# The small tail of an expert computed in front of its last full group of tokens

## The chip, the core and the metric

The kernel runs on one core of a Trainium2 chip. Its time is the device time of one execution in microseconds (us), the median of several runs. A core has five engines, each with its own queue of instructions that it works through in order: PE (matrix products; its weight loads are listed apart as PEld), DVE (vector operations), ACT (activation functions and copies), POOL (here nearly all indirect DMAs) and SP (here only DMAs). They wait for each other by semaphores, which a program sets from the data that instructions read and write.

## The reference

An attention with a local window and block summaries makes `x`, 3072 tokens of 512 numbers. Then a mixture of eight experts follows, of which each token uses two:

```python
logits = x @ w_gate
noisy_logits = logits + np.log1p(np.exp(x @ w_noise)) * noise
top2 = np.argpartition(-noisy_logits, 2, axis=1)[:, :2]
...
for e in range(E):
    for k in range(2):
        mask = top2[:, k] == e
        h = np.maximum(x[mask] @ w1[e], 0.0)
        out[mask] += top2_w[mask, k, None] * (h @ w2[e])
```

`w1[e]` is 512 x 1024 and `w2[e]` 1024 x 512. Only the experts matter here.

## The kernel before

The first 200 us or so compute the attention and the gate, which sorts the tokens of each expert into a list. After that the experts follow one another, in the order of how many tokens they have. Their numbers of places are fixed by `CAPS = (800, 832, 808, 800, 784, 776, 768, 768)`. All numbers are split in two float16 parts, high and low, so that a product of two matrices takes three passes: high by high, low by high, high by low.

From expert 2 on, an expert `e` goes through two stages:

- **First product** (`h = relu(x w1)`), `seven`: the expert's tokens are cut in two halves of `h = CAPS[e] // 2` columns, and `w1` in blocks, so that seven block products in place of eight make the result. One call `seven(e, i, u)` makes product `u` for block `i` with six matmuls (L1359), about 1 us. DVE and ACT add the products up (L1380 to L1387) and write `h` into the buffers `hth` and `htl` (high and low part, L1391 and L1394).
- **Second product** (`h w2`), `mm2_part`: for each group `c` of 128 tokens, 24 matmuls of 128 x 512 (L1431), about 5.2 us, into a PSUM buffer `pt` of which there are two. What lies beyond six groups of 128 is the **tail**, `c = LAST = 6`. Experts 3, 4 and 5 have tails of 32, 16 and 8 tokens (`four(e, c)` is true for them): 24 matmuls with 32 columns each, four side by side in the array (L1425), about 1.5 us for all, whose four partial sums then lie in four strips of 32 partitions. Experts 1 and 2 have larger tails (64 and 40 tokens), 6 and 7 have none.

`mm2_out` ends a group: one DVE instruction (L931) multiplies by the gate's weight and adds the tokens' old output rows, which `prev_gather` has fetched into one of three buffers `prev`; then POOL scatters the result to `out` (L90). For a tail of at most 32 tokens it is four DVE instructions, one for each strip, each adding to the one before (L920).

To have PE busy between two experts, `seven_head(n)` makes products 1 and 5 of the next expert `n = e + 1` ahead of the last turn of expert `e`. These twelve matmuls are called **the head** here. Product 1 writes the tile that PE rows call `o`, product 5 one called `h`.

The order of everything else is written out by hand: between PE's pieces of work the program calls `hook(t)`, and `on(t, f, ...)` puts a call at number `t`. In the second product the numbers are `32 + 3 * c` and `33 + 3 * c`, behind the first and the second pass of group `c`, and `34 + 3 * c`, behind its `mm2_out`. So a call's number fixes its place on its engine, and every engine keeps to that order. What the change touches:

- `plan_x(n, 3, 32, (44, 44, 44), (45, 45), (46, 46, 46, 46))` prepares the next expert's own tail for the first product: at most 16 rows of `x` are gathered, DVE makes three sums (L1292 to L1296, number 44), ACT the high parts (L1312, number 45), DVE the low parts (L1322, number 46, that is behind group 4), and for each part SP issues a DMA transpose (L1328) that puts it into the columns which the head reads too. The low parts of expert 4 lie in the tile `xl`, those of expert 5 in `xte`. Experts 6 and 7 have no tail, so nothing of this is done for them.
- `plan_w1(n, 3, 38, 47, 47, 48, 48, 49)` prepares the last quarter of the next expert's `w1`: four sums on DVE (L1339, number 47), the high parts on ACT (L1348, 47 and 48), the low parts on DVE (L1352, 48 and 49). They read staging buffers `stg`, four of them, which the next loads of weights reuse: the last two quarters of `w2` of expert `n` (L735 on SP, called early in the next expert), which ACT and DVE then split (L740, L758).
- `on(43, xs_gather, n + 1, 0)` and `on(47, xs_gather, n + 1, 1)` fetch token rows for the expert after next, by POOL.

The second product's loop before: groups 0 to 5 in order, then the tail, and the head ahead of whatever comes last.

Of the kernel before, what the change touches and what calls it, by code (L numbers as in the profile page):

```python
# [25 lines left out]
E, F = 8, 1024  # L26
# [37 lines left out]
def attn_moe(ctx, tc, qt, kt, vt, wgn, noise, w1, w2, out):  # L64
# [23 lines left out]
    def indirect(**kw):  # L88
        nc.gpsimd.memset(spacer, 0.0)
        return nc.gpsimd.indirect_dma_start(**kw)  # L90


    LAST = NCH - 1
# [74 lines left out]
    for i in range(3):  # L168
        m = const.tile([P, W], BF, name=f"mask{i}")
# [128 lines left out]
    def bank():  # L298
        return banks[0].tile([P, 1, 512], F32, name="h")
# [480 lines left out]
    def four(e, c):  # L780
        return c == LAST and CAPS[e] - LAST * P <= 32

    def tb_of(e, c):
        return TB0[:, c] if e == 0 and c < 3 else TB[:, e, c]
# [3 lines left out]
    def chunks(e):  # L788
        return -(-CAPS[e] // P)
# [83 lines left out]
    def prev_gather(e, c):  # L873
        n = min(P, CAPS[e] - c * P)
        pv = PREV[pi_[0] % len(PREV)]
        pi_[0] += 1
        if c == LAST and not four(e, c):
            g = indirect(
                out=pv[:, :HD], out_offset=None, in_=out2,
                in_offset=bass.IndirectOffsetOnAxis(ap=IL[:, e:e + 1], axis=0),  # L880
                bounds_check=2 * N - 1, oob_is_err=False)
        else:
            g = indirect(
                out=pv[:n], out_offset=None, in_=out,
                in_offset=bass.IndirectOffsetOnAxis(ap=tb_of(e, c)[:n, 0:1], axis=0),
                bounds_check=N - 1, oob_is_err=False)
        for o in ow.get(e, []):
            tc.declare_no_dep(g.ins, o.ins, reason="an expert's slots hold different tokens")
        ow.setdefault(e, []).append(g)
        return pv  # L890
# [20 lines left out]
    def mm2_out(e, c, py, pv):  # L911
        last = c == LAST
        if four(e, c):
            n = CAPS[e] - LAST * P
            y = late[0].tile([P, DM], F32, name="y", bufs=4)[:n]
            gw = tb_of(e, c).bitcast(F32)[:n, 1:2]
            for g in range(4):
                x = py[32 * g:32 * g + n]
                if g or pv is not None:
                    nc.vector.scalar_tensor_tensor(y, x, gw, y if g else pv[:n], op0=OP.mult, op1=OP.add)  # L920
                else:
                    nc.vector.tensor_scalar(y, x, gw, None, op0=OP.mult)
            y_scatter(e, c, y)
            return
        d = HD if last else DM
        y = late[0].tile([P, DM], F32, name="y", bufs=4)[:, :d]
        gw = (TL[:, e] if last else tb_of(e, c)).bitcast(F32)[:, 1:2]
        if pv is None:
            nc.vector.tensor_scalar(y, py[:, :d], gw, None, op0=OP.mult)
        else:  # L930
            nc.vector.scalar_tensor_tensor(y, py[:, :d], gw, pv[:, :d], op0=OP.mult, op1=OP.add)  # L931
        y_scatter(e, c, y)
# [287 lines left out]
    py = [bank()[:, 0] for c in range(3)]  # L1220
# [242 lines left out]
    def on(t, f, *a):  # L1463
        plan.setdefault(t, []).append((f, a))

    def hook(t):
        for f, a in plan.pop(t, []):
            f(*a)

    def plan_w1(n, p, t, *u):  # L1470
        on(t, w_load, n, p)
        on(u[0], w1_sums, n, p)
        for i in range(2):
            on(u[1 + i], w1_hi, n, p, i)
        for i in range(2):
            on(u[3 + i], w1_lo, n, p, i)
# [10 lines left out]

    for e in range(1, E):
        pv = []

        def prev():
            if len(pv) < chunks(e):
                pv.append(prev_gather(e, len(pv)))

        n = e + 1
        if e == 1:
            on(0, tail_ids)
            plan_x(n, 0, 0, (3, 3, 3), (4, 4), (5, 5, 5, 5))
            plan_x(n, 1, 1, (6, 6, 6), (7, 7), (8, 8, 8, 8))
            plan_w1(n, 0, 1, 9, 9, 10, 10, 10)  # L1500
            plan_w1(n, 1, 2, 11, 11, 12, 12, 12)
            plan_x(n, 2, 7, (13, 13, 13), (14, 14), (15, 15, 15, 15))
            plan_w1(n, 2, 11, 33, 33, 34, 34, 34)
            plan_x(n, 3, 12, (35, 35, 35), (36, 36), (37, 37, 37, 37))
            plan_w1(n, 3, 13, 38, 38, 39, 39, 39)
        else:
            for i, (a, b) in enumerate(((3, 4), (4, 7), (8, 14), (15, 21))):
                on(a, w_hi, e, 4 + i)
                on(b, w_lo, e, 4 + i)
            on(36, tail_next, e)  # L1510
            if n < E:
                plan_x(n, 0, None, (9, 11, 12), (10, 13), (15, 16, 18, 19))
                plan_x(n, 1, None, (22, 23, 25), (24, 27), (28, 29, 29, 31))
                plan_w1(n, 0, 8, 32, 32, 33, 33, 34)
                plan_w1(n, 1, 15, 35, 35, 36, 36, 37)
                plan_x(n, 2, 20, (38, 38, 38), (39, 39), (40, 40, 40, 40))
                plan_w1(n, 2, 35, 41, 41, 42, 42, 43)
                plan_x(n, 3, 32, (44, 44, 44), (45, 45), (46, 46, 46, 46))
                plan_w1(n, 3, 38, 47, 47, 48, 48, 49)
            if e > 2:  # L1520
                on(4, w_load, e, 6)
                on(4, w_load, e, 7)
        if n + 1 < E:
            on(40 if e == 1 else 43, xs_gather, n + 1, 0)
            on(42 if e == 1 else 47, xs_gather, n + 1, 1)
        if n < E:
            on(44, w_load, n, 4)
            on(44, w_load, n, 5)
        if e == 1:
            on(48, w_load, n, 6)  # L1530
            on(48, w_load, n, 7)
        for t in (17, 20, 23):
            on(t, prev)
        if e == 1:
            for half in range(2):
                for f in range(FC):
                    mm1(e, half, f)
                    hook(8 * half + f)
            for t in range(16, 32):
                hook(t)  # L1540
        else:
            hi, lo = seven(e, 0, 2)
            hi()
            lo()
            hook(3)
            seven(e, 0, 6)
            for t in range(4, 7):
                hook(t)
            for i in range(1, 5):
                if i < 4:  # L1550
                    seven(e, i, 1)
                    hook(7 * i)
                    seven(e, i, 5)
                    hook(7 * i + 1)
                h7 = seven(e, i - 1, 7)
                h7[0]()
                hook(7 * i + 2 if i < 4 else 28)
                if i < 4:
                    h2 = seven(e, i, 2)
                    h2[0]()  # L1560
                    h7[1]()
                    hook(7 * i + 3)
                    seven(e, i, 6)
                    h2[1]()
                    hook(7 * i + 4)
                else:
                    py = psum.tile([P, 512], F32, name="pt", bufs=2)
                    mm2_part(e, 0, py, 0, range(7), True, False)
                    h7[1]()
                    hook(29)  # L1570
                h3 = seven(e, i - 1, 3)
                h3[0]()
                hook(7 * i + 5 if i < 4 else 30)
                h4 = seven(e, i - 1, 4)
                h4[0]()
                h3[1]()
                h4[1]()
                hook(7 * i + 6 if i < 4 else 31)
        for c in range(chunks(e)):
            if c == chunks(e) - 1 and n < E:  # L1580
                seven_head(n)
            if c or e == 1:
                py = psum.tile([P, 512], F32, name="pt", bufs=2)
                for i, k in enumerate((0, 2, 1)):
                    if e == 1:
                        mm2_pass(e, c, py, k, 1)
                    else:
                        mm2_part(e, c, py, k, range(FC), i == 0, i == 2)
                    if i < 2:
                        hook(32 + 3 * c + i)  # L1590
            else:
                for k in (2, 1):
                    mm2_part(e, 0, py, k, range(7), False, False)
                    hook(33 - k // 2)
                for k in (0, 2, 1):
                    mm2_part(e, 0, py, k, (7,), False, k == 1)
            mm2_out(e, c, py, pv[c])
            prev()
            hook(34 + 3 * c)
        for t in range(60):  # L1600
            hook(t)
# [104 lines left out]
```

## Time and profile before

| | |
|---|---|
| median of 3 runs | 644.59 us (644.32 to 644.63) |
| the profiled execution | 642.6 us, of which the span of instructions is 640.8 |
| granted PE clock, mean | 0.997 |
| 24 matmuls of a group, L1431 | 5.2 us |
| 24 matmuls of a tail of at most 32 tokens, L1425 | 1.4 us |
| four instructions L920 on DVE | 3.1 us |
| one L931 on DVE | 0.75 us |
| the five passages from an expert to the next, 2 to 3 up to 6 to 7 | near 332, 394, 455, 516 and 572 us of the span |

The profile is of one execution. A timeline's row gives the start of a group of like instructions, its length, and what they were; in square brackets stands how long the engine sat idle ahead of it, and what ended that. Matmuls are pipelined: one of 128 x 512 is listed with 0.38 us, while the next starts 0.22 after it. So the distance of starts says how PE moves, and the length of a row ends a little after the next has begun.

### The profile page before, as it was taken

How to read it: one execution, taken by the hardware profiler on the slowest of the kernel's cores; microseconds unless marked ns; L12 is line 12 of the kernel's file. 1: busy time of each engine (PE TensorE's matmuls, PEld its weight loads, DVE VectorE, ACT ScalarE, POOL GpSimd, SP SyncE). 2: the span in 40 equal slices, each digit the busy share in tenths (PEclk: the TensorE clock that was granted, in tenths of full speed). 3: DMA queues.
4: the chain of work that ended last, by engine and by line, in shares of the span. 5: the costliest groups of instructions: out<-in, count | busy, mean ns of one | idle time of the engine just before them, and what ended most of it. 6: DMA issues, size and time to landing. Idle time of an engine off the chain costs nothing.

```text
span 640.8 us, 14153 instructions
## 1 busy us (share of the span) xinstructions
PE 622.5 (97%) x5295; PEld 358.8 (56%) x5295; DVE 481.3 (75%) x1039; ACT 315.9 (49%) x692; POOL 249.0 (39%) x432
## 2 busy tenths in 40 slices
PE   8999999999999999999999999999999999999995
PEld 7778777765654544555455544554554455445542
DVE  5768999889796797188868887987898679757410
ACT  4868988941253553075437534654464255425200
POOL 4442224203254324532573266336523532333041
PEclk9999999999999999999999999999999999999998
DMA  9999986788379976547886597759677767763021
GB/s 308 333 292 351 292 266 201 222 318 250 118 217 171 253 186 170 211 122 140 209 265 152 131 228 245 181 133 250 201 189 156 218 205 166 182 198 105 3 96 51
DMA packets 123708, 127.93 MB, mean 200 GB/s; under 512 B 83242, under 2 KB 86674, under 8 KB 123630
## 3 DMA queue, kind: packets, MB, share of 16 engines
q1 hardware_dynamic: 111838, 90.66, 53.3%
q0 software_dynamic: 11792, 36.27, 18.0%
q8 instruction: 44, 0.72, 0.5%
q14 instruction: 34, 0.28, 0.1%
HBM read 81.85 MB, written 25.61 MB: 168 GB/s over the span
## 4 chain that ended last, share of the span: by engine, by line
PE 82%; DVE 6%; issue 3%; DMA 3%; ACT 2%; POOL 1%; SPq 1%; POOLq 0%; DVEq 0%; ACTq 0%
PE pt L1431 29%; PE h L1359 16%; PE h L854 8%; PE pt L909 5%; PE pt L341 3%; PE pt L1359 3%; PE o L1359 3%; PE s L318 3%; PE o L354 3%; PE h L909 2%; DMA xte<-x 2%; PE pt L378 1%; PE o L246 1%; DVE y L920 1%; DVE htl L1394 1%
## 5 line engine op out<-in xcount | busy, mean ns | idle before, releaser
L90 POOL DMA_INDIRECT out_dram<-y,tb x52 | 69.3, 1333 | 169.4 <-DVE y L931 131.6
L90 POOL DMA_INDIRECT xg<-xd,tb x54 | 60.1, 1112 | 118.1 <-DVE dsc L653 32.3
L1431 PEld LDWEIGHTS <-hth 128*128 128x128 f16 x576 | 56.4, 98 | 66.7
L931 DVE SCALAR_TENSOR_TENSOR y<-pt,tb,prev 128x512 f32<-128x512 f32 x42 | 31.5, 750 | 67.4 <-PE pt L1431 49.8
L1359 PEld LDWEIGHTS <-w1h 128*128 128x128 f16 x504 | 48.9, 98 | 38.0 <-issue 4.1
L1431 PE MATMUL pt<-w2h,hth 128*128 128x512 f16 x288 | 69.0, 379 | 0.0
L1431 PE MATMUL pt<-w2h,htl 128*128 128x512 f16 x288 | 69.0, 379 | 0.0
L1431 PE MATMUL pt<-w2l,hth 128*128 128x512 f16 x288 | 69.0, 379 | 0.0
L1359 PEld LDWEIGHTS <-w1l 128*128 128x128 f16 x504 | 49.3, 98 | 34.9
L90 POOL DMA_INDIRECT prev<-out_dram,tb x45 | 52.4, 1165 | 23.7 <-issue 12.8
L333 ACT ACTIVATE p<-s,nm 128x120 f32<-128x120 f32 x192 | 51.0, 376 | 0.8
L854 PE MATMUL h<-xte,w1h 128*128 128x384 f16 (+2 forms) x248 | 48.9, 336 | 1.1 <-DMA xte<-x 1.1
L1431 PEld LDWEIGHTS <-htl 128*128 128x128 f16 x288 | 28.2, 98 | 34.0
L1348 ACT ACTIVATE w1h<-stg 128x768 f16<-128x768 f32 (+1 forms) x24 | 22.7, 944 | 37.9 <-DVE stg L1339 37.9
L1391 ACT ACTIVATE hth<-h 128x384 f16<-128x384 f32 (+4 forms) x48 | 23.8, 496 | 35.6 <-PE h L1359 35.6
L1348 ACT ACTIVATE w1l<-stg 128x768 f16<-128x768 f32 (+1 forms) x24 | 22.5, 942 | 37.2 <-DVE stg L1339 37.2
L1359 PE MATMUL h<-xte,w1h 128*128 128x384 f16 (+4 forms) x180 | 39.7, 329 | 0.7 <-DVE h L1385 0.4
L1359 PE MATMUL h<-xte,w1l 128*128 128x384 f16 (+4 forms) x180 | 39.7, 329 | 0.0
L1339 DVE TENSOR_TENSOR stg<-stg 128x256 f32<-128x256 f32 x96 | 36.2, 419 | 0.8
L854 PEld LDWEIGHTS <-w1h 128*128 128x128 f16 x256 | 24.7, 98 | 20.5 <-issue 2.2
L1312 ACT ACTIVATE x<-xt 128x512 f16<-128x512 f32 (+2 forms) x44 | 26.3, 625 | 19.6 <-issue 17.3
L1394 DVE SCALAR_TENSOR_TENSOR htl<-h,hth 128x384 f16<-128x384 f32 (+4 forms) x48 | 26.3, 562 | 11.8 <-ACT hth L1391 11.5
(301 smaller groups left out, 1292.0 us busy)
## 6 DMA issues: line engine op xcount, KB each, us to landing
stg<-in_w_dram SPq DMA_DIRECT2D x64, 512.0 KB
q<-in_qt_dram SPq DMA_DIRECT2D x24, 256.0 KB
xd<-x SPq DMA_DIRECT2D x24, 256.0 KB
out_dram<-xg SPq DMA_DIRECT2D x8, 768.0 KB
kb<-in_kt_dram SPq DMA_DIRECT2D x6, 768.0 KB
hth<-in_vt_dram SPq DMA_DIRECT2D x12, 260.0 KB
htl<-in_vt_dram SPq DMA_DIRECT2D x16, 195.0 KB
ve<-in_vt_dram SPq DMA_DIRECT2D x12, 260.0 KB
```

Source lines behind the costliest of these rows:

```text
L90: return nc.gpsimd.indirect_dma_start(**kw)
L333: nc.scalar.activation(PE_[t][:, a, hp, :], SC[t][:, a, hp, :], AF.Exp, bias=NM[t][:, 1, a, hp:hp + 1], scale=0.125)
L854: nc.tensor.matmul(ph[:, :n], w1_of(w, wn, c, f), x[:, xo + c, c0:c1], start=(k == 0), stop=(k == 11))
L909: nc.tensor.matmul(py, hx[:, f, c * P:c * P + P], wv[:, f, :], start=st, stop=sp)
L931: nc.vector.scalar_tensor_tensor(y, py[:, :d], gw, pv[:, :d], op0=OP.mult, op1=OP.add)
L1312: nc.scalar.activation(t[:r, c:c + k], src, AF.Copy)
L1339: nc.vector.tensor_tensor(o, x, y, op=op)
L1348: nc.scalar.activation(hi, x, AF.Copy, scale=W1S)
L1359: nc.tensor.matmul(ph[:, :h], w[:, la, a, P * j:P * j + P], x[:, j, :h], start=start and k == 0, stop=k == 5, skip_group_check=True)
L1391: nc.scalar.activation(hh[:, f, t], src, AF.Relu)
L1394: nc.vector.scalar_tensor_tensor(hl[:, f, t], src, 0.0, hh[:, f, t], op0=OP.max, op1=OP.subtract)
L1431: nc.tensor.matmul(py, x, wv[:, f, :], start=st, stop=sp, skip_group_check=True)
```

## The change

For experts whose tail has at most 32 tokens (3, 4 and 5), the last two turns of the second product change places: groups 0, 1, 2, 3, 4, then the tail, then group 5. The head of the next expert stays ahead of the last turn, which is now group 5. The fetches of old output rows follow the new order. And for these three experts the numbers of the last quarter of `w1` are written anew, since the tail's numbers (50, 51) now come ahead of those of group 5 (47, 48): its sums and high parts sit in the tail's turn, its low parts in that of group 5.

```diff
     for e in range(1, E):
         pv = []
+        turns = list(range(chunks(e)))
+        if chunks(e) > LAST and four(e, LAST):
+            turns[-2:] = turns[:-3:-1]
 
         def prev():
             if len(pv) < chunks(e):
-                pv.append(prev_gather(e, len(pv)))
+                pv.append(prev_gather(e, turns[len(pv)]))
...
-                plan_w1(n, 3, 38, 47, 47, 48, 48, 49)
+                plan_w1(n, 3, 38, *((50, 50, 51, 47, 48) if LAST in turns[:-1] else (47, 47, 48, 48, 49)))
...
-        for c in range(chunks(e)):
-            if c == chunks(e) - 1 and n < E:
+        for m, c in enumerate(turns):
+            if c == turns[-1] and n < E:
                 seven_head(n)
...
-            mm2_out(e, c, py, pv[c])
+            mm2_out(e, c, py, pv[m])
```

The order on PE where it passes from expert 3 to expert 4, before: the end of group 5 (L1431), the first and the last of the head's matmuls (L1359), the start of the tail (L1425).

```order
L1431 LDWEIGHTS htl
L1431 MATMUL pt<-w2h_321,htl 128x512
L1359 LDWEIGHTS w1h_319
L1359 MATMUL o<-xte,w1h_319 128x392
...
L1359 MATMUL h<-xl,w1h_319 128x392
L1425 LDWEIGHTS hth
L1425 MATMUL pt<-w2h_321,hth 32x512
```

And the same place after the change:

```order
L1425 LDWEIGHTS htl
L1425 MATMUL pt<-w2h_321,htl 32x512
L1359 LDWEIGHTS w1h_319
L1359 MATMUL o<-xte,w1h_319 128x392
...
L1359 MATMUL h<-xl,w1h_319 128x392
L1431 LDWEIGHTS hth
L1431 MATMUL pt<-w2h_321,hth 128x512
```

The head now stands between the tail and group 5, where it stood between group 5 and the tail.

The order on DVE at the same place, as a difference (`-` before, `+` after), from the low parts of expert 4's tail (L1322) and the sums of its `w1` (L1339) to the first results of expert 4:

```order
 L1322 TENSOR_TENSOR x<-xt,x 16x512 x2
 L1339 TENSOR_TENSOR stg<-stg 128x256 x4
+L920 SCALAR_TENSOR_TENSOR y<-pt,tb,prev_2965 32x512
+L920 SCALAR_TENSOR_TENSOR y<-pt,tb,y 32x512 x3
 L1352 SCALAR_TENSOR_TENSOR w1l_2957<-stg,w1l_2957 128x768
-L931 SCALAR_TENSOR_TENSOR y<-pt,tb,prev_2965 128x512
 L1352 SCALAR_TENSOR_TENSOR w1l_2957<-stg,w1l_2957 128x1024
-L920 SCALAR_TENSOR_TENSOR y<-pt,tb,prev_2966 32x512
-L920 SCALAR_TENSOR_TENSOR y<-pt,tb,y 32x512 x3
+L931 SCALAR_TENSOR_TENSOR y<-pt,tb,prev_2966 128x512
 L1394 SCALAR_TENSOR_TENSOR htl<-o,hth 128x392
```

The tail's four L920 moved up behind the sums, and the L931 of group 5 moved to where they stood; L1322 and L1339 stand where they did. The orders of ACT and SP are the same before and after. On POOL the tail's scatter moved ahead of the two gathers of number 47.

## The prediction

> **What bounds the kernel now.** I read the page first, for the engine that carries the span, then PE's timeline at the places that the change touches, for gaps in it, then DVE's and SP's there, for what ends the gaps. From the page:
>
> ```profile
> PE 622.5 (97%) x5295; PEld 358.8 (56%) x5295; DVE 481.3 (75%) x1039; ACT 315.9 (49%) x692; POOL 249.0 (39%) x432
> ```
>
> PE works for 97% of the span. The change adds and removes no instruction, so it can only move time by changing where PE waits. It touches experts 3, 4 and 5, whose tails are 32, 16 and 8 tokens; the others have a tail of 64 or 40, or none. So three places matter: where PE passes from expert 3 to 4, from 4 to 5, from 5 to 6. PE's timeline at the first (columns: start, length, instruction; in square brackets the idle time before it):
>
> ```profile
> 387.11 1.89 PE L1431 MATMUL pt<-w2h,hth 128*128 128x512 f16 x8
> ...
> 392.29 0.83 PE L1359 MATMUL o<-xte,w1h 128*128 128x392 f16 x4
> 392.96 0.49 PE L1359 MATMUL o<-xl,w1h 128*128 128x392 f16 x2
> ...
> 393.95 0.49 PE L1359 MATMUL h<-xl,w1h 128*128 128x392 f16 x2
> ...
> 395.79 0.84 PE L1359 MATMUL o<-xte,w1h 128*128 128x392 f16 x4
> ...
> 399.44 0.49 PE L1359 MATMUL h<-xl,w1l 128*128 128x392 f16 x2
> 400.12 0.82 PE L1359 MATMUL h<-xte,w1h 128*128 128x392 f16 x4 [0.18 <-DVE h L1385]
> ...
> 405.76 0.49 PE L1359 MATMUL o<-xl,w1h 128*128 128x392 f16 x2
> 406.36 0.82 PE L1359 MATMUL h<-xte,w1h 128*128 128x392 f16 x4
> ```
>
> In order: group 5 from 387.11, the head of expert 4 from 392.29, the tail of expert 3, and from 395.79 the rest of expert 4. Four matmuls take 0.67 (392.29 to 392.96), so two take 0.33. Against that pitch PE loses 400.12 - 399.44 - 0.33 = 0.35 us at the first gap and 406.36 - 405.76 - 0.33 = 0.27 at the second. The same two gaps at the other places:
>
> ```profile
> 448.18 0.59 PE L1431 MATMUL pt<-w2h,hth 128*128 128x512 f16 x2
> ...
> 455.00 0.49 PE L1359 MATMUL h<-xte,w1h 128*128 128x388 f16 x2
> ...
> 460.46 0.49 PE L1359 MATMUL h<-xte,w1l 128*128 128x388 f16 x2
> 461.16 0.82 PE L1359 MATMUL h<-w2l,w1h 128*128 128x388 f16 x4 [0.22 <-DVE h L1385]
> ...
> 466.74 0.49 PE L1359 MATMUL o<-xte,w1h 128*128 128x388 f16 x2
> 467.38 0.82 PE L1359 MATMUL h<-w2l,w1h 128*128 128x388 f16 x4
> ...
> 521.26 0.49 PE L1359 MATMUL h<-xl,w1l 128*128 128x384 f16 x2
> 522.00 0.81 PE L1359 MATMUL h<-xte,w1h 128*128 128x384 f16 x4 [0.25 <-DVE h L1385]
> ...
> 527.52 0.49 PE L1359 MATMUL o<-xl,w1h 128*128 128x384 f16 x2
> 528.19 0.81 PE L1359 MATMUL h<-xte,w1h 128*128 128x384 f16 x4 [0.18 <-DVE htl L1394]
> ```
>
> That is 0.37 + 0.31 at the second place and 0.41 + 0.34 at the third: 0.62 + 0.68 + 0.75 = **2.05 us** in all. DVE at the first place says why:
>
> ```profile
> 387.31 0.75 DVE L931 SCALAR_TENSOR_TENSOR y<-pt,tb,prev 128x512 f32<-128x512 f32 x1 [1.82 <-PE pt L1431]
> 387.98 1.02 DVE L1322 TENSOR_TENSOR x<-xg,x 16x512 f16<-16x512 f32 x2
> 388.94 1.27 DVE L1322 TENSOR_TENSOR x<-xt,x 16x512 f16<-16x512 f32 x2
> 390.14 1.53 DVE L1339 TENSOR_TENSOR stg<-stg 128x256 f32<-128x256 f32 x4
> ...
> 395.91 0.74 DVE L920 SCALAR_TENSOR_TENSOR y<-pt,tb,prev 32x512 f32<-32x512 f32 x1 [1.53 <-PE pt L1425]
> 396.68 2.31 DVE L920 SCALAR_TENSOR_TENSOR y<-pt,tb,y 32x512 f32<-32x512 f32 x3
> ...
> 399.50 0.56 DVE L1385 TENSOR_TENSOR h<-h,p 128x392 f32<-128x392 f32 x1
> ```
>
> The four L920 of the tail hold DVE from 395.91 to 398.99, at the very time when expert 4's first results come; L1385, for which PE waits, ends only at 400.06.
>
> **What the change takes away.** The four L920 now stand behind the sums L1339 and need only the tail, which PE finishes early. DVE is with the sums until 391.67; then 3.08 us of L920 bring it to 394.75, and the two L1352 to about 397 (an estimate: SP's two L735 loads, whose row stands below, each go as one L1352 ends, at 392.57 and 2 us later, with an L931 of 0.75 between them). What stays behind the last group is one L931 (0.75), not four L920. Expert 6 has no tail, so the trace already holds a transition of just this form, from group 5 straight into expert 7 (two rows of PE's timeline, one of DVE's):
>
> ```profile
> 576.83 0.81 PE L1359 MATMUL o<-w2h,w1h 128*128 128x384 f16 x4
> ...
> 580.73 0.81 PE L1359 MATMUL h<-w2l,w1h 128*128 128x384 f16 x4
> ...
> 579.30 0.56 DVE L1385 TENSOR_TENSOR h<-h,p 128x384 f32<-128x384 f32 x1
> ```
>
> 24 matmuls fill 576.83 to 580.73, and the one that depends on L1385 starts without a gap: L1385 ended at 579.86, 0.87 before. So I count all six gaps as gone: -2.05. Bounds: nothing (0), and not more than 2.05, since no other gap there belongs to DVE.
>
> **What the change brings forward.** The head of the next expert used to start after group 5. Now group 5 stands behind it, so the head comes one group earlier and directly after the tail. The tail's 24 matmuls take 395.79 - 393.95 - 0.33 = 1.51. So the head of expert 4 would start at 387.11 + 1.51 = 388.62 in place of 392.29: 3.67 earlier. Its inputs do not come earlier. The head multiplies columns that hold the next expert's own tail, and their low parts are made by L1322, behind the L931 of group 4 on DVE, and then turned by SP's transposes:
>
> ```profile
> 389.03 2.37 SPq L1328 DMA_TRANSPOSE xl<-x  x2
> 392.57 2.21 SPq L735 DMA_DIRECT2D stg<-in_w_dram  x2
> ...
> 450.08 2.36 SPq L1328 DMA_TRANSPOSE xte<-x  x2
> ```
>
> Both transposes stand at the same place in DVE's and SP's order as before; group 4's end releases them, and that does not move. They are issued from 389.03 to 391.40. When do they land? The trace has no row for that, so I asked the DMA view in windows of 0.3 us for q1, the queue of SP's transfers (columns: packets, MB, share). From 392.00, from 392.30, and for the next expert from 453.30:
>
> ```profile
> q1 hardware_dynamic: 31, 0.00, 6.8%
> ...
> q1 hardware_dynamic: 2, 0.00, 0.3%
> ...
> q1 hardware_dynamic: 10, 0.00, 1.5%
> ```
>
> These are the last small packets of the second transposes; I put the landing at the middle of the last window at the first place, 392.45, and just behind the last one at the second, 453.65.
>
> Now the wait. The head's last two matmuls, which read the second low part, come 393.95 - 392.29 = 1.66 after its start: wanted at 388.62 + 1.66 = 390.28, there at 392.45, so PE stands **2.2 us** (most of it already at the fifth matmul, wanted at 389.29, whose part is issued at 389.03). For expert 5: start 448.18 + 1.51 = 449.69, wanted at 451.35, landed 453.65: **2.3 us**. Expert 6 has no tail and so no such pieces: 0. Sum +4.5. Bounds of each stall: at least 1.1, if the data were there the moment SP had finished issuing (391.40, 452.44); at most 3.67, since before the head read them at 393.95 and 455.00 without a wait. I take the packets, as the nearest thing to a landing that the trace has.
>
> By the Trainium skill, "DMA: Bandwidth & Descriptors", section "Anatomy of one DMA — SWDGE (gpsimd) path", a transfer has a fixed cost of about 2.0 us, most of it the receipt of the last write. Counted as an estimate from the end of the issue, that would be 393.40 and 454.44, 3.1 us for each stall, and 648.8 for the kernel; the trace's packets are over some 0.9 us earlier, so I do not take it.
>
> **What is hidden.** Edits with one answer: other work covers them. The rows that say how long, from ACT's and DVE's timelines:
>
> ```profile
> 400.37 1.05 ACT L740 ACTIVATE w2h<-stg 128x1024 f16<-128x1024 f32 x1
> ...
> 414.78 0.68 DVE L1292 TENSOR_TENSOR xt<-xg 128x512 f32<-128x512 f32 x1
> ```
>
> - The tail's scatter on POOL now waits for L920 (to about 394.8) ahead of two gathers for the expert after next, which start near 396 and not right behind group 4's scatter, some five microseconds later. Their reader on DVE comes at 414.78. Without that cover the delay would be the cost.
> - The last group's old output rows are fetched one turn later, still with the tail, the head and the whole group's 24 matmuls ahead of their use; the tail's, one turn earlier.
> - The two L735 loads on SP wait for the L1352, so they start near 395.7 and 396.9, not 392.57. ACT converts the first at 400.37, and PE's stall pushes that to 402.6: about 7 us for 512 KB. If it came later than that, ACT would hold back expert 4's next results.
> - The last group needs its PSUM buffer back from group 4 (L931 over at 388.06), and PE asks for it after the head: free.
>
> **The sum.** -2.05 + 4.5 = +2.45. The profiled execution took 642.6 (span 640.8 and 1.8 around it), so 645.0 there. The three timed runs have their median at 644.59, 2.0 above that execution; I carry the difference over: 644.59 + 2.45 = **647.0**. A change of 0.2% (1.3 us) is about what a measurement of this kernel can tell from none, so this would just show as slower.
>
> **The rivals.**
> - *Faster: the gaps go and the head finds its inputs.* 644.59 - 2.05 = 642.5. It decides at the landing: the second low parts would have to be there by 390.28 and 451.35. For it speaks only that before nothing waited for them; against it, that DVE is not done making them before 390.2. Chance 0.07.
> - *No change: the stall is short.* Data there at the end of issue: 2.2 - 2.05 = +0.2, 644.8. The packets speak against it. With the lower edge of my forecast, 0.15 for a time within 0.2%.
> - *The relief does not come*: L1352 and L931 hold DVE as long as L920 did. 644.59 + 4.5 = 649.1. Expert 6 speaks against it. 0.06.
> - *The clock falls in the stall.* The windows of the end (columns: PE, PEld, DVE, ACT, POOL busy, granted clock, DMA share, GB/s):
>
> ```profile
> 633.00:634.00 1.00, 0.43 (x2) 0.00 (x0) 0.54 (x1) 0.00 (x0) 0.00 (x0) 1.00 0.04 12
> ...
> 637.00:638.00 1.00, 0.00 (x0) 0.00 (x0) 0.00 (x0) 0.00 (x0) 0.00 (x0) 0.50 0.05 20
> ```
>
> PE ends 0.43 into the first row; the rows left out have 1.00 up to 636 and 0.87 behind it. So it took over 2.5 us without a matmul. Mine are 2 us, so this needs a stall near its upper bound. If the clock then came back only after as long at half speed, each stall would cost 1.3 us more: 647.0 + 2.6 = 649.6. Chance 0.04. The Trainium skill, "TensorE: Matmul & The Clock Gate", section "What's actually happening", has the clock halve after an idle window of about 3.4 us; by that rule, as by these rows, two microseconds are too few.
>
> That the change does not do what it says can be left out: the rows of the engines' order above show it done at all three places.
>
> **How the numbers follow.** The forecast has 0.68 for itself beyond the 0.2% bound, and the two dearer rivals 0.10, so slower 0.78, same 0.15, faster 0.07. The range goes from 645.0 (stalls of 1.2 each) to 649.2 (stalls of 3.3 each, or the relief missing), which leaves out the faster case, the clock and the last ends of the landing: under 2 in 10.
>
> **What would show it.** Right: PE waits of about 2 us in front of a head's matmuls at two places only, for experts 4 and 5, ended by transposes; none at expert 6; no PE gap ended by L1385 or L1394 in experts 4 to 6; L920 directly behind the sums. Wrong: a head that runs through at 388.6, which makes it 642.5; L1385 still late; or a PE wait for a converted weight or an old output row, which I count as hidden.

## The result, and the profile after

The changed kernel takes **649.8 us** (median of 6 runs, 648.05 to 651.98) against 644.46 (643.43 to 645.11, 6 runs) for the kernel before, measured beside it: ratio 1.0086 [1.0059, 1.0113]. It is slower, as forecast, but by 5.3 us and not by 2.45, and the time lies above the range.

The profiled execution took 648.98 us, its span 647.2, at a mean granted clock of 0.993. The row of the engines on its page:

```profile
PE 625.8 (97%) x5295; PEld 360.4 (56%) x5295; DVE 481.2 (74%) x1039; ACT 315.8 (49%) x692; POOL 254.8 (39%) x432
```

The work is the same, but PE is listed as busy for 3.3 us more: the same matmuls took longer. The view of PE's waits, from 380 to 530 us, has two rows (what waited for what: us in total, times, the longest):

```profile
PE o L1359 <- DMA xl<-x: 3.1, 1, 3.1
PE o L1359 <- DMA xte<-x: 3.0, 1, 3.0
```

Two waits, for experts 4 and 5, ended by the transposes; none at expert 6, and no row for L1385 or L1394: those gaps are gone. PE's timeline at the first place and, behind the last "...", at the second:

```profile
387.52 0.84 PE L1359 MATMUL o<-xte,w1h 128*128 128x392 f16 x4
391.41 0.49 PE L1359 MATMUL o<-xl,w1h 128*128 128x392 f16 x2 [3.05 <-DMA xl<-x]
391.74 0.83 PE L1359 MATMUL h<-xte,w1h 128*128 128x392 f16 x4
392.40 0.67 PE L1359 MATMUL h<-xl,w1h 128*128 128x392 f16 x2
392.87 3.44 PE L1431 MATMUL pt<-w2h,hth 128*128 128x512 f16 x8
396.15 1.89 PE L1431 MATMUL pt<-w2l,hth 128*128 128x512 f16 x8
...
399.60 0.83 PE L1359 MATMUL o<-xte,w1h 128*128 128x392 f16 x4
...
403.25 0.49 PE L1359 MATMUL h<-xl,w1l 128*128 128x392 f16 x2
403.58 0.83 PE L1359 MATMUL h<-xte,w1h 128*128 128x392 f16 x4
...
452.88 0.83 PE L1359 MATMUL o<-w2h,w1h 128*128 128x388 f16 x4
456.75 0.49 PE L1359 MATMUL o<-xte,w1h 128*128 128x388 f16 x2 [3.04 <-DMA xte<-x]
...
458.66 2.98 PE L1431 MATMUL pt<-w2h,hth 128*128 128x512 f16 x8
...
464.93 0.82 PE L1359 MATMUL o<-w2h,w1h 128*128 128x388 f16 x4
```

Four things can be read here. The head's fifth matmul is due 0.67 behind 387.52 and starts at 391.41: PE is held up by 391.41 - 387.52 - 0.67 = 3.22 us (at the second place 3.21). The four matmuls from 391.74 and the last two run without another wait, so the second low part no longer holds anything up. The pitch from 403.25 to 403.58 is 0.33: the gap for L1385 is gone. And the first eight matmuls of group 5 take 396.15 - 392.87 = 3.28 us from start to start, where eight took 1.73 before, a third of 5.18. The reason for the last reading is the granted clock, in the windows of the first place (columns as in the prediction: us, busy time of PE, PEld, DVE, ACT, POOL, then the granted clock):

```profile
389.00:390.00 1.00, 0.00 (x0) 0.00 (x0) 0.97 (x4) 0.00 (x0) 1.00 (x1) 1.00 0.76 168
...
391.00:392.00 1.00, 0.59 (x4) 0.38 (x4) 0.96 (x2) 0.71 (x2) 0.00 (x0) 1.00 0.57 209
392.00:393.00 1.00, 1.00 (x7) 0.55 (x6) 0.94 (x2) 0.42 (x1) 0.00 (x0) 0.79 0.00 0
...
394.00:395.00 1.00, 1.00 (x3) 0.29 (x2) 1.00 (x2) 0.00 (x0) 1.00 (x1) 0.50 0.00 0
...
396.00:397.00 1.00, 1.00 (x6) 0.40 (x5) 0.00 (x0) 0.00 (x0) 0.76 (x3) 1.00 0.89 317
```

While PE stands, the clock is whole. It halves at 392.58 (0.79 is 0.42 us at half), when PE has been at work again for over a microsecond, and is back at 396.0.

What released PE is in the chain of work that ended last (start, length, what):

```profile
386.89 1.03 DVE x L1322 x3
387.92 3.45 DMA xl<-x
...
391.41 0.49 PE o L1359 x2
```

DVE makes the low part, SP issues its transpose at 387.92, PE is released 3.45 us later, at 391.37, and goes on at 391.41. DVE's own timeline there:

```profile
390.48 0.73 DVE L920 SCALAR_TENSOR_TENSOR y<-pt,tb,prev 32x512 f32<-32x512 f32 x1
391.25 2.31 DVE L920 SCALAR_TENSOR_TENSOR y<-pt,tb,y 32x512 f32<-32x512 f32 x3
...
401.81 0.56 DVE L1385 TENSOR_TENSOR h<-h,p 128x392 f32<-128x392 f32 x1
```

The four L920 are over at 393.56, and L1385 ends at 402.37, 1.21 us before PE's matmul at 403.58.

**Accounting.** Executions differ by some microseconds in the attention ahead of the experts, so I compare one stretch: from the first L1431 of expert 2's second product to the point at expert 7 where PE has passed the last of the three changed places. It is 280.02 us before (296.81 to 576.83) and 287.76 after: **+7.74**. Worked out from the rows: held up 3.22 + 3.21 = 6.43; slow clock, as the head and group 5 take 399.60 - 387.52 = 12.08 against 1.99 + 5.18 = 7.17 in the kernel before, 4.91 more, of which 3.22 are the hold-up: 1.69 at each place, 3.38; relief -2.05. The sum is +7.76.

### The profile page after: what moved, and what is told of

It reads as the page before. It is cut to its first block, busy times and chain, and to the rows that moved or that the text cites. A ratio compares the mean times of both kernels' runs of the same rounds, so it can differ in the third digit from the quotient of the medians.

```text
span 647.2 us, 14154 instructions
## 1 busy us (share of the span) xinstructions
PE 625.8 (97%) x5295; PEld 360.4 (56%) x5295; DVE 481.2 (74%) x1039; ACT 315.8 (49%) x692; POOL 254.8 (39%) x432
## 4 chain that ended last, share of the span: by engine, by line
PE 90%; DVE 5%; ACT 2%; issue 1%; DMA 1%; POOL 0%; POOLq 0%; DVEq 0%
PE pt L1431 29%; PE h L1359 19%; PE h L854 10%; PE pt L909 7%; PE pt L1359 4%; PE o L1359 4%; PE pt L341 3%; PE o L354 3%; PE s L318 2%; PE h L909 2%; PE o L246 1%; PE pt L378 1%; DVE nm L325 1%; ACT p L333 1%; PE s L308 1%
## 5 line engine op out<-in xcount | busy, mean ns | idle before, releaser
L90 POOL DMA_INDIRECT out_dram<-y,tb x52 | 74.4, 1431 | 164.1 <-DVE y L931 134.6
L1431 PEld LDWEIGHTS <-hth 128*128 128x128 f16 x576 | 57.1, 99 | 68.6 <-issue 3.9
L931 DVE SCALAR_TENSOR_TENSOR y<-pt,tb,prev 128x512 f32<-128x512 f32 x42 | 31.4, 749 | 72.8 <-PE pt L1431 62.0
L1359 PEld LDWEIGHTS <-w1h 128*128 128x128 f16 x504 | 49.0, 98 | 42.6 <-issue 8.6
L1431 PE MATMUL pt<-w2h,hth 128*128 128x512 f16 x288 | 71.7, 390 | 0.0
L1431 PE MATMUL pt<-w2h,htl 128*128 128x512 f16 x288 | 69.0, 379 | 0.0
L1431 PE MATMUL pt<-w2l,hth 128*128 128x512 f16 x288 | 69.0, 379 | 0.0
L1359 PEld LDWEIGHTS <-w1l 128*128 128x128 f16 x504 | 49.3, 98 | 34.9
L1431 PEld LDWEIGHTS <-htl 128*128 128x128 f16 x288 | 28.2, 98 | 34.0
L1359 PE MATMUL h<-xte,w1h 128*128 128x384 f16 (+4 forms) x180 | 40.0, 332 | 0.0
L1359 PE MATMUL h<-xte,w1l 128*128 128x384 f16 (+4 forms) x180 | 39.7, 329 | 0.0
L1339 DVE TENSOR_TENSOR stg<-stg 128x256 f32<-128x256 f32 x96 | 36.2, 419 | 0.8
L1394 DVE SCALAR_TENSOR_TENSOR htl<-h,hth 128x384 f16<-128x384 f32 (+4 forms) x48 | 26.6, 563 | 12.4 <-ACT hth L1391 12.1
```

The source lines that it names most:

```text
L1339: nc.vector.tensor_tensor(o, x, y, op=op)
L1359: nc.tensor.matmul(ph[:, :h], w[:, la, a, P * j:P * j + P], x[:, j, :h], start=start and k == 0, stop=k == 5, skip_group_check=True)
L1394: nc.vector.scalar_tensor_tensor(hl[:, f, t], src, 0.0, hh[:, f, t], op0=OP.max, op1=OP.subtract)
L1431: nc.tensor.matmul(py, x, wv[:, f, :], start=st, stop=sp, skip_group_check=True)
```

## The experiments

Two theories at first. **A**: the transposes hold up the head, and the clock falls on top because PE stands. **B**: the head is held up, but the slow matmuls have a cause of their own, such as the moved work of DVE and POOL beside group 5. All edits are against the changed kernel. The first four kernels ran with the kernel before at 645.93 (median of 29 runs), the next four at 644.98 (27 runs); "traced" is by how much the stretch of the accounting is longer than the 280.02 us of the kernel before.

**The inputs earlier.** The numbers of the next expert's tail are moved up by one group of the second product.

```diff
-                plan_x(n, 3, 32, (44, 44, 44), (45, 45), (46, 46, 46, 46))
+                g3 = 3 if LAST in turns[:-1] else 0
+                plan_x(n, 3, 32, (44 - g3,) * 3, (45 - g3,) * 2, (46 - g3,) * 4)
```

> The changed kernel with one thing more: for experts 3 and 4 the next expert's own tail is prepared one group earlier (sums 41, high parts 42, low parts 43 in place of 44, 45, 46), so that its low parts are issued to SP near the end of group 3 and have one more group's time to land. Theory (the head waits for these transposes, and the clock falls because of that wait): the two waits of 3.05 us are gone, group 5 takes 5.2 us both times at a granted clock of 1.00, and what is left is the relief of 2.05 us: some 0.3% faster than before. Rival (moving the tail itself makes group 5 slow, by other traffic or by the switch between tile shapes): group 5 still takes 6.2 to 6.7 us and the kernel stays slower than before.

Measured: 643.41 us (642.41 to 645.74, 12 runs), ratio 0.9969 [0.9951, 0.9987]; traced -1.48. PE's timeline:

```profile
390.41 0.84 PE L1359 MATMUL o<-xte,w1h 128*128 128x392 f16 x4
...
392.43 0.49 PE L1359 MATMUL h<-xl,w1h 128*128 128x392 f16 x2 [0.18 <-DMA xl<-x]
392.76 1.89 PE L1431 MATMUL pt<-w2h,hth 128*128 128x512 f16 x8
```

The head takes 392.76 - 390.41 = 2.35 us, 0.36 over its 1.99, for the second low part; 0.24 at the second place. That is the difference to -2.05. The matmuls of group 5 run at their usual 1.89 with the moved L920 beside them. So the late inputs are what made the changed kernel slower, and B has no support here.

**The head back behind group 5.** The tail keeps its new place, and the head moves behind the last group's matmuls where an expert's tail is moved and the next expert has one.

```diff
-            if c == turns[-1] and n < E:
+            wait = LAST in turns[:-1] and tail(min(n, E - 1))
+            if c == turns[-1] and n < E and not wait:
                 seven_head(n)
...
+            if c == turns[-1] and n < E and wait:
+                seven_head(n)
             mm2_out(e, c, py, pv[m])
```

> The changed kernel, but for experts 3 and 4 the head of the next expert stands behind group 5's matmuls, where it starts at the same time as before the change (the tail keeps its new place). Theory (the head is too early for its inputs): no wait for transposes, no fall of the clock; the head's own products then have only each other as cover for ACT's copies, at most some 0.3 us of new gaps at each of the two places; so 1.4 to 2.05 us faster than before, about 0.3%. Rival (the tail's place is what costs): slower than before by 3 us or more, with the time lost in group 5 or behind the tail.

Measured: 643.24 us (639.79 to 647.07, 12 runs), ratio 0.9963 [0.9939, 0.9987]; traced -2.05.

```profile
398.96 0.83 PE L1359 MATMUL o<-xte,w1h 128*128 128x392 f16 x4
...
400.95 0.83 PE L1359 MATMUL o<-xte,w1h 128*128 128x392 f16 x4
...
404.60 0.49 PE L1359 MATMUL h<-xl,w1l 128*128 128x392 f16 x2
404.93 0.83 PE L1359 MATMUL h<-xte,w1h 128*128 128x392 f16 x4
```

The head takes 1.99, the gap for L1385 is 0.33, a plain pitch, and the view of waits has no row for PE between 260 and 600 us. This is the change without its harm: the relief as the prediction had it, to the hundredth. By its ratio, with the whole interval below 1, it is faster than the kernel before.

**PE kept at work while the transposes land.** At experts 3 and 4, N matmuls whose results nothing reads go between the tail and the head (they write the last group's PSUM buffer, and its first matmul overwrites them).

```diff
-            if c == turns[-1] and n < E:
+            if c == turns[-1] and n < E and LAST in turns[:-1] and tail(n):
+                py = psum.tile([P, 512], F32, name="pt", bufs=2)
+                for i in range(13):
+                    nc.tensor.matmul(py, ones, HT[0][:, 0, 0:512], start=True, stop=True, skip_group_check=True)
                 seven_head(n)
+            elif c == turns[-1] and n < E:
+                seven_head(n)
...
```

> The changed kernel with 13 matmuls of 128x512 more in front of the head of experts 4 and 5, whose results nothing reads: they take 13 x 0.216 = 2.8 us, nearly the 3.05 us that PE stands there. Theory (the clock halves because PE stands idle for three microseconds): the head's low parts still arrive at the same time, so the wait shrinks to some 0.3 us and the time to the head's end does not change, but the granted clock stays at 1.00 and group 5 takes 5.2 us: 3.4 us less than the changed kernel in these two places, so about 4.3 us above before in place of 7.7. Rival (group 5 is slow by contention for memory, or by reading what is just being written): group 5 stays at 6.2 to 6.7 us, and the time stays that of the changed kernel.

Measured with 13: 648.68 us (647.55 to 651.49, 9 runs), ratio 1.0049 [1.0022, 1.0075]; traced +4.17.

```profile
393.68 0.83 PE L1359 MATMUL o<-xte,w1h 128*128 128x392 f16 x4
...
395.93 1.89 PE L1431 MATMUL pt<-w2h,hth 128*128 128x512 f16 x8
...
401.11 0.83 PE L1359 MATMUL o<-xte,w1h 128*128 128x392 f16 x4
```

Group 5 takes its usual 401.11 - 395.93 = 5.18 us. Group 5 still starts only when the head has its data, so the delay stays; what is gone against the changed kernel is 7.74 - 4.17 = 3.57, the slow clock and a little more. A is borne out: the clock fell because PE stood, and it cost about 1.7 us at each place.

> The same with 6 such matmuls, 1.3 us: PE then stands idle for some 1.75 us in place of 3.05. Theory of the prediction (about 2 us of standing is too short for the clock to fall): the granted clock stays at 1.00, group 5 takes 5.2 us, and the time is that of the run with 13. Rival (a shorter standing also does it): the clock falls for some 3 us as in the changed kernel, and the time is that of the changed kernel.

Measured with 6: 650.13 us (646.53 to 652.27, 9 runs), ratio 1.0065 [1.0039, 1.009]; traced +4.25, without a fall of the clock.

```profile
PE o L1359 <- DMA xl<-x: 1.8, 1, 1.8
PE o L1359 <- DMA xte<-x: 1.6, 1, 1.6
```

So stands of 1.8 and 1.6 us did not lower the clock in this execution. The mean clocks of its nine timed runs go from 0.993 to 0.998, and five are at 0.994 or less; the profiled one had 0.997. In some of the others it probably fell, here or elsewhere.

**The changed kernel again.**

> The changed kernel unaltered, on the chip and beside the runs of before that the other runs of this set share. Its first trace had 7.7 us more than before's between expert 2's second product and expert 7's first, while the timed medians were 5.3 apart. Theory (two waits of 3.2 us, two falls of the clock of 1.7 us, less 2.05 of relief): the trace shows both waits and both falls again, 287.8 us for that stretch within 0.3, and a ratio near 1.010. Rival (a fall of the clock in the first trace by chance): one or both of the falls are missing here, and the ratio is nearer to 1.007.

Measured: 650.19 us (647.56 to 654.45, 10 runs), ratio 1.0074 [1.0045, 1.0103]; traced +8.93, waits 3.0 and 3.0. The clock fell at both places again, and the first time it stayed low for twice as long, to 399.76, so the stretch is 1.2 us longer than expected. The ratio is nearer to the 1.007 of the rival, though neither fall is missing; what stays open, below, comes back to that. One window of the first place:

```profile
398.00:399.00 1.00, 1.00 (x4) 0.39 (x3) 0.00 (x0) 0.00 (x0) 0.83 (x2) 0.50 0.75 248
```

**The tail moved at expert 5 alone**, where the next expert has none.

```diff
-        if chunks(e) > LAST and four(e, LAST):
+        if chunks(e) > LAST and four(e, LAST) and not tail(e + 1):
             turns[-2:] = turns[:-3:-1]
```

> The change for expert 5 alone, whose successor has no tail; experts 3 and 4 keep the order of before. Theory: no wait of the head, no fall of the clock, and only the two gaps of 0.41 and 0.34 us behind expert 5 go: 0.75 us less than before in the stretch from expert 2's second product to expert 7 (279.3 in place of 280.0), a time that measurement can hardly tell from before (ratio 0.999). Rival (a tail in front of the last group costs something by itself): that stretch is not shorter than before, and group 5 of expert 5 takes more than 5.2 us.

Measured: 643.81 us (641.38 to 649.43, 12 runs), ratio 0.9984 [0.9955, 1.0013], which tells nothing of so small an effect; traced -0.76.

```profile
521.95 0.49 PE L1359 MATMUL h<-xl,w1l 128*128 128x384 f16 x2
522.27 0.81 PE L1359 MATMUL h<-xte,w1h 128*128 128x384 f16 x4
```

The gap of 0.41 at this point is now a pitch of 0.32, and no wait comes in its place: the third place's share of the relief, -0.75, stands by itself.

**Four matmuls in the stand.**

> The changed kernel with 4 matmuls of 128x512 more (0.86 us) in front of the head of experts 4 and 5, so that PE stands for some 2.2 us there, as long as the prediction had it. The prediction's view (2 us is too short for the clock to fall): granted clock 1.00 throughout in the trace, mean clocks of the runs as in the run with 13 such matmuls (0.996 to 0.998), about 4.3 us above before. Rival (about 2 us is enough, depending on where it falls): mean clocks of most runs at 0.993 to 0.995 as in the changed kernel, and 6 us or more above before.

Measured: 649.81 us (645.75 to 653.86, 12 runs), ratio 1.0069 [1.0042, 1.0097]; traced +6.05. PE waited 2.17 us at the first place and 2.20 at the second, and yet the clock stayed whole at the first and fell at the second. Eleven of its twelve timed runs have mean clocks of 0.993 to 0.995, as the rival had it, though their median is 4.8 us above before and not 6. The length of the stand alone does not decide.

**The kernel before again**, for the stretch.

> The kernel before, unaltered, for a second trace: how well does a stretch of the trace repeat? Every theory: 280.0 us from expert 2's second product to expert 7's first within 0.3, the six gaps of 0.27 to 0.41 us again, and differences between executions only ahead of expert 1.

Measured: one run, 644.37 us; the stretch is 280.02 again, with the gaps in their places. So the stretch repeats well enough to tell a few tenths.

**What decides whether the clock falls.** In the trace's record of the granted clock, falls within one execution lie whole multiples of one length apart: in the changed kernel 392.59, 457.44 and 645.17 us, which is 19.0 and 74.0 times 3.413. It looks like a grid that runs on regardless of the kernel, with the clock set anew at each line. Laid over the ten traces, it had every stretch with 1.38 us or less of PE work followed by one at half clock, and none with 1.56 or more. Four new traces test it: the changed kernel unaltered, and the fill kernel with 2, 4 and 5 matmuls (the edit above, with another N).

> The changed kernel unaltered, for one more trace. In the ten traces so far all falls of the granted clock within one trace lie whole multiples of 3.413 us apart, and of the stretches of 3.413 us that this grid marks out, every one in which PE was busy for 1.38 us or less was followed by a stretch at half clock, and none with 1.56 or more. Theory of the grid: the same here, for each place and for the rest of the trace; PE stands some 3.2 us at each of the two places, so a place escapes only where the stand is cut by a line of the grid into two parts that both leave over 1.4 us of work, about 1 time in 5 for each place. Rival (the length of the stand decides): the clock falls both times, wherever the stand lies in the grid of the other falls.

> The changed kernel with 2 matmuls, whose results nothing reads, between the tail and the head at experts 4 and 5. PE then stands some 2.6 to 2.8 us at each place. Theory of the grid: a stretch of 3.413 us, counted from any fall in this trace, with at most 1.38 us of PE work is followed by half clock, one with 1.56 or more is not; about 2 falls in 3 places. Rival (length alone decides, with 2.2 enough as at the second place of fill4): both places fall.

> The same with 4 matmuls, once more. PE stands some 2.2 to 2.4 us at each place. Theory of the grid: as above; about every second place falls, those whose stretch between two lines of the grid holds at most 1.38 us of PE work, and no others. Rival (length alone): both places alike, since the stands are alike.

> The same with 5 matmuls. PE stands some 2.0 to 2.2 us at each place, only just more than the 2.03 us that a stretch must stand idle (3.41 less 1.38). Theory of the grid: a fall only where nearly the whole stand lies within one stretch, under every second place; any stretch with 1.56 us of work or more leaves the clock whole. Rival (length alone, with an end between 1.8 and 2.2): both places alike.

The times, of one run each beside one of the kernel before at 643.43: 650.75, 653.68, 649.2 and 650.18 us. The windows of the grid, columns as above, first of the unaltered kernel, with waits of 2.91 and 3.11 us:

```profile
389.82:393.23 3.41, 0.50 (x4) 0.19 (x2) 3.34 (x8) 0.96 (x1) 2.04 (x4) 1.00 0.69 221
393.23:396.64 3.41, 3.41 (x12) 1.46 (x10) 3.34 (x5) 1.08 (x3) 1.13 (x1) 0.50 0.01 4
```

With 2, waits of 2.54 and 2.46 us (the second place had 0.95 and fell too):

```profile
394.17:397.58 3.41, 1.25 (x8) 0.77 (x8) 3.31 (x7) 1.54 (x2) 1.23 (x2) 1.00 0.52 165
397.58:400.99 3.41, 3.41 (x10) 1.22 (x9) 2.94 (x4) 0.50 (x1) 2.16 (x1) 0.50 0.11 25
```

With 4, both places, waits of 2.13 and 2.08 us:

```profile
389.83:393.24 3.41, 1.52 (x8) 0.69 (x7) 3.38 (x8) 0.51 (x1) 2.48 (x4) 1.00 0.75 192
393.24:396.65 3.41, 3.16 (x17) 1.66 (x17) 3.30 (x6) 1.52 (x3) 0.68 (x1) 1.00 0.15 54
454.68:458.09 3.41, 1.32 (x9) 0.69 (x8) 3.31 (x8) 1.53 (x2) 1.47 (x2) 1.00 0.56 171
458.09:461.50 3.41, 3.41 (x10) 1.24 (x9) 3.17 (x4) 0.49 (x1) 1.92 (x1) 0.50 0.07 13
```

With 5, waits of 1.90 and 1.92 us, both places:

```profile
391.46:394.88 3.42, 2.58 (x25) 1.02 (x18) 3.39 (x9) 0.00 (x0) 3.12 (x3) 1.00 0.69 195
394.88:398.29 3.41, 2.35 (x13) 1.26 (x13) 3.30 (x6) 2.04 (x3) 0.13 (x2) 1.00 0.29 99
456.32:459.73 3.41, 1.49 (x10) 0.69 (x8) 3.34 (x8) 0.93 (x1) 2.08 (x4) 1.00 0.69 219
```

The rows with 1.32 us of work or less are followed by half clock, those with 1.49 or more are not, and two stands of equal length went two ways with 4. That pair and the one of the first kernel with 4 are what speaks against the length: the unaltered kernel and the one with 2 fell both times, the one with 5 neither time, which either theory allows. At the first place with 5 a line of the grid cuts the stand, and both parts leave over 2.3 us of work. A fall elsewhere narrows the edge (the kernel with 2 matmuls, in its attention, by chance):

```profile
66.49:69.90 3.41, 1.47 (x22) 1.23 (x20) 1.40 (x2) 0.14 (x1) 0.78 (x2) 1.00 0.85 220
69.90:73.31 3.41, 3.41 (x38) 2.45 (x37) 2.06 (x6) 3.38 (x12) 0.17 (x1) 0.50 0.96 301
```

So in 14 traces the edge lies between 1.47 and 1.49 us of 3.41, in busy time as the trace lists it. The first fill kernel with 4 fits too: a line at 392.60 left 2.17 and 2.48 us of work to either side of the first stand, while the second lay whole in one stretch with 1.21. The theory that the length decides has fallen.

The traced differences then have one rule:

| kernels | stretches at half clock at the two places | traced |
|---|---|---|
| 5, 6 and 13 matmuls in the stand | 0 | +4.25, +4.25, +4.17 |
| 4 matmuls, two traces | 1 | +6.05, +5.90 |
| the changed kernel, two of its three traces; 2 matmuls | 2 | +7.74, +7.50; +7.50 |
| the changed kernel, third trace | 3, with 0.9 us of them while PE stood | +8.93 |

Each stretch at half clock costs half its length, 1.7 us, and the rest, 4.2, is the delay less the relief.

**What stays open.** The timed medians differ by 5.3 and 5.2 us (by the intervals 3.8 to 7.3 and 2.9 to 6.6), the three traces by 7.5 to 8.9. A stand of 3.2 us escapes where the grid's line cuts it so that neither part idles for 3.41 - 1.48 = 1.93: by an estimate that takes every position as equally likely, (2 x 1.93 - 3.2) / 3.41, 1 time in 5. On average that makes 4.2 + 2 x 0.8 x 1.7 = 6.9, inside the first interval and above the second. The clocks of the second set bear the estimate out: their mean is 0.9927 over the ten runs of the changed kernel and 0.9966 over the 27 of before, which is 2.6 us more of lost clock, 1.5 stretches at half clock. So missing falls seem to explain a part only. The timed difference lies below the traced one in the other kernels of the two sets too, by up to 1.4 us (2.75 against 4.17 with 13 matmuls, -2.5 against -1.48 with the inputs earlier). What makes up the rest, perhaps the attention part, was not settled.

## Why the prediction was right and wrong

- **Relief, right.** Forecast -2.05; traced -2.05 with the head out of the way, and -0.76 for the third place alone against its 0.75.
- **Which places wait, and for what, right.** Two waits, for experts 4 and 5, ended by the transposes, none at expert 6.
- **What is hidden, right.** Beside the two waits for transposes no PE wait is listed from 260 to 600 us in the changed kernel, and none at all is left once the head stands behind group 5: neither the converted weights nor the old output rows nor the PSUM buffer were late.
- **The size of the stall, wrong.** The term was 2.2 + 2.3 = 4.5; it measured 3.22 + 3.21 = 6.43. I took the last small packets of the second transposes as the landing, and priced the head's last two matmuls by it. PE stood at the fifth matmul, for the first low part. The packets of q1 in the changed kernel (DMA view: packets, MB, share) show what is missing, from 390.5, 390.8, 391.1 and 391.4, each for 0.3 us:

```profile
q1 hardware_dynamic: 18, 0.02, 20.3%
...
q1 hardware_dynamic: 1, 0.00, 2.0%
...
q1 hardware_dynamic: 15, 0.00, 2.6%
...
q1 hardware_dynamic: 17, 0.00, 2.8%
```

The trace's record of single packets is finer: it has two groups of 32 packets of 4 bytes, from 390.40 to 390.61 and from 391.28 to 391.60, each behind 16 larger packets. That the groups are the two transposes is read off their order; the record has no names. PE goes on at 391.41, 0.8 us behind the first group, and the readers of the second low part run at 392.40, 0.8 behind the second group, without a wait. So packets are over well before the engine that waits is let go, and both parts were later than I had them. For the first, 3.45 behind its issue at 389.03 in the trace of before would be 392.48, against 389.29 when it was wanted: 3.2, as measured. The upper bound of 3.67 held. Nearer was the estimate that I set aside, 3.1 each. It rests on the Trainium skill, "DMA: Bandwidth & Descriptors", section "Anatomy of one DMA — SWDGE (gpsimd) path", whose fixed cost of about 2.0 us is given for transfers that POOL issues. Here SP issues them, and from the end of the first issue (half of 2.36 behind 387.92) to PE's start it was 2.3; so the nearness is in part luck, all the more as I had counted from the second issue.
- **The clock, wrong.** The rival "the clock falls in the stall" had 0.04, since two microseconds were "too few" beside the 2.5 at the kernel's end. That stand was longer than I read it: the 0.87 dates the fall at 636.74, 3.3 us behind PE's last work. The rival's price, 1.3 each, was near the measured 1.69. What failed is the inference that the length of a stand must reach a fixed bound: the end of the kernel shows how long one stand lasted, not how short one may be. The clock goes by how much of a fixed stretch of 3.41 us PE works. By the estimate above even the 2.2 us that I forecast would have lowered it about every second time: it escapes in (2 x 1.93 - 2.2) / 3.41 of the positions, 0.49.

The two errors add 1.9 and, in the trace, 3.4 us to the forecast of +2.45, which makes the +7.74 of the stretch; the timed runs show 5.3 of it. The stalls alone would have stayed inside the range: 644.59 - 2.05 + 6.43 = 649.0. That the rival's time, 649.6, is near the measured 649.8 is partly chance, as it has the shorter stalls.

## What to carry to other kernels

Before work is moved forward on the engine that bounds a kernel, ask whether its inputs move too; here they did not, and it cost 6.4 us of standing. Take each input's whole chain, to the release of its first reader, and price the first matmul that needs it, not the last. A short stand of PE costs more than its length when it fills enough of one clock stretch; here stands of 2.1 to 2.2 us were enough twice and not enough twice. Where the order of two late pieces can be swapped, put the one whose inputs are old in front: the tail ahead of group 5 with the head behind it keeps the relief at 0.9963 [0.9939, 0.9987] of the time before (the inputs moved up, at 0.9969, cannot be told from it).

## What was not expected of the hardware

The granted clock is set on a grid: in seven traces with more than one fall, the twelve distances from a trace's first fall are whole multiples (19 to 170) of 3.4133 us, to a thousandth of it. While whole, it halves behind a stretch with at most 1.47 us of PE work (26 of 26 that lie whole in the span, in 14 traces) and not behind one with 1.49 or more. So the fall comes up to a stretch later than its cause, when PE already works again. The low clock lasted one stretch where PE worked for 3.16 us or more of it, and a second one in the one case ahead of the kernel's end with less: in the changed kernel's second trace the first low stretch, from 392.93, held 0.9 us of standing, and the next was low too. The Trainium skill, "TensorE: Matmul & The Clock Gate", section "What's actually happening", says that the window is free-running and some 3.4 us long, and there the traces agree. It has the clock fall after an idle window, and there they differ, as 1.47 us of work in a window did not keep it up.

From the start of SP's issue of a transpose of 16 rows to the matmul that waits for it, 3.3 to 3.5 us passed in all 16 waits of the eight traces in which PE stood at both places (3.49 at the first: 387.92 to 391.41).
